# Query-key sums moved from TensorE to accumulating DMAs, and a third GLU block ahead of the down projections

## The chip, the cores and the metric

The kernel runs on one core of a Trainium2 chip. The metric is the device time of one execution in microseconds (us), taken as the median of several executions on the same chip. The profiled execution also has a *span*, from the first to the last instruction, which is about 2 us shorter than the device time of the same execution. Where this text compares stages it uses spans; where it compares kernels it uses device times. The engines are TensorE (PE in the profile; PEld is its weight load), VectorE (DVE), ScalarE (ACT), GpSimd (POOL) and SyncE (SP). POOLq and SPq are the DMA queues that GpSimd and SyncE issue to.

## The reference

One token block of 2048 rows and 640 columns is normalised and then goes through two branches, whose results are added to the input.

```python
def reference(A_x, A_wqkv, A_wo, B_x, B_w_gate, B_w_up, B_w_down):
    xn = layernorm(A_x)                       # [1, 2048, 640], bf16
    # A: 32 heads of 20 columns, a window of 8 keys, 2 apart, backwards
    q, k, v = split_heads(xn @ A_wqkv)        # H = 32, Dh = 20
    idx  = pos[:, None] - 2 * arange(8)       # mask: idx >= 0
    logits = einsum("bhsd,bhswd->bhsw", q, k[idx]) * 20 ** -0.5
    attn = softmax(where(mask, logits, -1e9))
    a = merge_heads(einsum("bhsw,bhswd->bhsd", attn, v[idx])) @ A_wo
    # B: gated linear unit, F = 1536
    b = ((xn @ B_w_gate) * (xn @ B_w_up)) @ B_w_down
    return A_x + a + b                        # B_x is not used
```

## The kernel before

TensorE does the QKV projections, then the GLU products ("gate-up": 4 blocks of 512 rows, each 24 groups of 5 matmuls, 1.08 us a group), then the *down sums*: for 128 rows, twelve matmuls of HT with WD and five of VO with WO into one bank. VectorE does the attention. A head's 20 columns lie as 5 chunks times 4 neighbouring partitions. For each *pair* of window positions (4 pairs for each half of the sequence, 8 in all) VectorE multiplies the 5 chunks of queries and keys, adds two of the five onto two others, and TensorE sums the remaining three chunks and the four partitions with a 0/1 matrix G. ScalarE evicts the result into LOG.

```python
def qk_steps(h, p, s):                        # VectorE, one pair
    kept, tmp = SL[s], TMP                    # kept: 3 chunks, tmp: 2 chunks, 2 window positions each
    ...
    return [(..., prod(kept, 0, NKC)),        # 6144 columns
            (..., prod(tmp, NKC, NCH)),       # 4096 columns
            (..., lambda: ... tensor_tensor(a, a, b, ALU.add))]

def qk_logits(h, batch):                      # TensorE: 12 matmuls a pair
    for p, s in batch:
        for c in range(NKC):
            for q in range(NSB):
                ... e.matmul(o, G[:], x, start=(c == 0), stop=(c == NKC - 1), ...)
    for p, s in batch:
        ... e.activation(o, i, ACT.Copy, scale=SCALE)      # LOG <- PS
    ...
```

Instructions are emitted in program order by a small static scheduler. VectorE's steps are emitted one after the other, and TensorE's "fill" (projections, GLU, down sums) is emitted between them by a modelled clock. The instructions of one engine stand in its queue in the order of emission; waits are inserted from data dependences.

```python
add_gu(0); add_gu(1); add_dn(0); add_gu(2); add_dn(1); add_gu(3); add_dn(2); add_dn(3)   # fill, in this order

batch(0, [pair(0, 0), pair(0, 1)])
batch(0, [pair(0, 2), pair(0, 3)])
headA, restA = softmax_steps(0)               # half A
...
b0 = pair(1, 0)
settle()
for it in headA: step(it)
batch(1, [b0, pair(1, 1)])
for it in restA: step(it)
attn_move(0)
batch(1, [pair(1, 2), pair(1, 3)])            # then WD and WO are loaded over the product buffers
...
pv(0); settle(); headB; pv(1); restB; attn_move(1); pv(2) ... pv(7)   # attention times values, 256 rows each
```

A GLU group of gate and up leaves HT and USX, each evicted from PSUM by ScalarE, and VectorE multiplies HT by USX. There are six USX buffers for this, and six PSUM banks while G needs the other two (eight after the change). If VectorE stands, ScalarE soon has no USX buffer to evict into, and TensorE soon has no bank to write.

## Time and profile before

| | before |
|---|---|
| device time, median of 3 | 262.39 us (262.02 to 262.39) |
| profiled span | 260.7 us |
| TensorE busy | 255.6 us, 98% |
| VectorE busy | 216.1 us, 83% |
| ScalarE busy | 107.3 us, 41% |
| GpSimd busy | 6.7 us, 3% |

The top of the profile page of the kernel before: span, busy time of each engine, and TensorE's busy share in 40 equal slices, in tenths (9 is 90% or more).

```profile
span 260.7 us, 4018 instructions
...
PE 255.6 (98%) x1669; PEld 150.7 (58%) x1669; DVE 216.1 (83%) x240; ACT 107.3 (41%) x193; POOL 6.7 (3%) x13
...
PE   7999999899999999999999999999999999999996
```

TensorE is busy nearly everywhere, so it is taken to be the bound: what is taken from TensorE is gained as long as nothing makes it wait.

TensorE's timeline around the first block of G matmuls (start, duration, engine, line, operation, tiles, count; in brackets the idle time before it and what ended it):

```profile
47.61 0.83 PE L485 MATMUL PS<-SL,G 128*32 128x512 f16 x12
49.35 0.83 PE L485 MATMUL PS<-SL,G 128*32 128x512 f16 x12 [0.91 <-DVE SL L475]
50.11 2.14 PE L424 MATMUL PS<-XNT,WQKV 128*128 128x512 bf16 x9
```

The block takes 50.11 - 47.61 = 2.50 us of TensorE, 0.91 of them idle. The three other blocks of 24 take 1.44, 1.41 and 1.41 us, in all 6.8 us.

Three windows of 10 us (window; its length; busy time and count on PE, PEld, DVE, ACT, POOL; the granted TensorE clock, 1.00 is full; the share of the DMA engines; GB/s):

```profile
100.00:110.00 10.00, 10.00 (x49) 4.51 (x47) 10.00 (x9) 5.66 (x10) 0.00 (x0) 1.00 0.16 50
110.00:120.00 10.00, 10.00 (x65) 4.33 (x64) 9.53 (x11) 5.82 (x11) 0.00 (x0) 1.00 0.71 240
150.00:160.00 10.00, 10.00 (x51) 4.75 (x50) 9.93 (x5) 4.43 (x8) 0.00 (x0) 1.00 0.79 198
```

The one on-chip transfer in the kernel before, in the table of DMA issues (how many, size, median us from issue to landing):

```profile
ATB<-LOG SPq DMA_DIRECT2D x32, 128.0 KB, 2.6
```

### The profile page before, as it was taken

The page shows a single profiled execution, that of the slowest core. Times are in us where ns is not written, and L with a number is a line of the kernel's source. Part 1 is how long each engine was busy: PE and PEld are TensorE (multiplying, and loading weights), DVE is VectorE, ACT ScalarE, POOL GpSimd, SP SyncE. Part 2 cuts the span into 40 slices and gives each one's busy share as a digit, 9 for nine tenths or more (in the row PEclk, how much of TensorE's full clock was granted, in tenths as well). Part 3 has the DMA queues.
Part 4 walks back from the last instruction along what each step waited for, and adds up shares of the span by engine and source line. Part 5 has one row for each costly group of instructions (what it writes and reads, how often), then busy time and mean ns, then how long its engine had stood idle before and what let it go on. Part 6 is the DMA issues. An engine that isn't in the chain of part 4 may idle for free.

```text
span 260.7 us, 4018 instructions
## 1 busy us (share of the span) xinstructions
PE 255.6 (98%) x1669; PEld 150.7 (58%) x1669; DVE 216.1 (83%) x240; ACT 107.3 (41%) x193; POOL 6.7 (3%) x13
## 2 busy tenths in 40 slices
PE   7999999899999999999999999999999999999996
PEld 3899855354554444444467744446774444777775
DVE  5799889999999999998847999999999999422221
ACT  3565558555657555565630035551004555000000
POOL 2000050000200000000000000000000000000000
DMA  6968889400000275065001376000311000021301
GB/s 202 326 136 148 100 226 402 156 3 0 0 3 0 50 206 144 0 208 219 3 0 57 97 199 175 0 4 0 99 54 50 0 3 0 27 74 53 101 28 50
DMA packets 21922, 23.46 MB, mean 90 GB/s; under 512 B 9872, under 2 KB 19472, under 8 KB 21904
## 3 DMA queue, kind: packets, MB, share of 16 engines
q1 hardware_dynamic: 21760, 23.04, 31.2%
q8 instruction: 13, 0.21, 0.3%
q10 hardware_dynamic: 144, 0.16, 0.2%
q14 instruction: 5, 0.04, 0.0%
HBM read 14.42 MB, written 2.62 MB: 65 GB/s over the span
## 4 chain that ended last, share of the span: by engine, by line
PE 80%; DVE 14%; SPq 2%; DMA 2%; ACT 1%; issue 1%
PE PS L577 40%; PE PS L608 28%; PE PS L424 10%; DVE SL L467 3%; SPq L283 2%; DVE XNS L371 2%; PE PS L485 2%; DVE STATS L354 2%; DVE SL L475 2%; DVE TMP L467 2%; DVE STATS L348 2%; DMA XST<-in_A_x_dram 2%; DVE MV L360 1%; DVE SD L369 1%; ACT KH L451 0%
## 5 line engine op out<-in xcount | busy, mean ns | idle before, releaser
L577 PE MATMUL PS<-XNT,WG 128*128 128x512 bf16 x240 | 59.6, 379 | 0.0
L577 PE MATMUL PS<-XNT,WU 128*128 128x512 bf16 x240 | 59.6, 379 | 0.0
L608 PE MATMUL PS<-WD,HT 128*128 128x320 bf16 (+1 forms) x396 | 57.6, 295 | 0.0
L579 ACT ACTIVATE HT<-PS 128x512 bf16<-128x512 f32 x48 | 28.7, 598 | 58.2 <-PE PS L577 58.2
L608 PEld LDWEIGHTS PS<-WD,HT 128*128 128x128 bf16 x396 | 38.1, 98 | 14.7
L551 DVE TENSOR_TENSOR PVB<-VO,ATB 128x10240 f16<-128x10240 bf16 x8 | 43.9, 5488 | 0.1
L424 PE MATMUL PS<-XNT,WQKV 128*128 128x512 bf16 x200 | 43.9, 379 | 0.0
L612 DVE TENSOR_TENSOR FOUT<-PS,XR 128x320 bf16<-128x320 f32 (+1 forms) x33 | 15.5, 477 | 30.4 <-PE PS L608 30.1
L577 PEld LDWEIGHTS PS<-XNT,WU 128*128 128x128 bf16 x240 | 23.4, 98 | 28.5 <-issue 0.4
L577 PEld LDWEIGHTS PS<-XNT,WG 128*128 128x128 bf16 x240 | 23.4, 98 | 28.2 <-issue 0.4
L579 ACT ACTIVATE USX<-PS 128x512 bf16<-128x512 f32 x48 | 28.7, 597 | 22.2 <-PE PS L577 20.8
L424 PEld LDWEIGHTS PS<-XNT,WQKV 128*128 128x128 bf16 x200 | 23.3, 118 | 20.2 <-issue 0.8
L546 DVE TENSOR_TENSOR PVB<-PVB 128x5120 f16<-128x5120 f16 (+1 forms) x16 | 34.4, 2150 | 0.0
L467 DVE TENSOR_TENSOR SL<-QH,KH 128x6144 f16<-128x6144 bf16 x8 | 26.8, 3352 | 1.4 <-ACT KH L451 1.4
L608 PE MATMUL PS<-WO,VO 128*128 128x320 bf16 (+1 forms) x165 | 27.1, 295 | 0.0
L582 DVE TENSOR_TENSOR HT<-HT,USX 128x512 bf16<-128x512 bf16 x48 | 18.5, 417 | 4.2 <-ACT USX L579 4.2
L608 PEld LDWEIGHTS PS<-WO,VO 128*128 128x128 bf16 x165 | 15.9, 98 | 5.9
L475 DVE TENSOR_TENSOR SL<-SL,TMP 128x4096 f16<-128x4096 f16 x8 | 18.3, 2290 | 0.2
L467 DVE TENSOR_TENSOR TMP<-QH,KH 128x4096 f16<-128x4096 bf16 x8 | 18.4, 2302 | 0.0
L430 ACT ACTIVATE VO<-PS 128x512 bf16<-128x512 f32 x20 | 11.9, 597 | 9.8 <-PE PS L424 9.8
L437 PE MATMUL PS<-XNT,WQKV 128*128 128x128 bf16 x200 | 12.6, 220 | 0.2
L437 PEld LDWEIGHTS PS<-XNT,WQKV 128*128 128x128 bf16 x200 | 11.6, 118 | 1.2 <-DVE XNT L394 0.5
(49 smaller groups left out, 137.8 us busy)
## 6 DMA issues: line engine op xcount, KB each, us to landing
ATB<-LOG SPq DMA_DIRECT2D x32, 128.0 KB, 2.6
XR<-in_A_x_dram SPq DMA_DIRECT2D x16, 160.0 KB, 2.3
XST<-in_A_x_dram SPq DMA_DIRECT2D x15, 160.0 KB, 3.9
out_dram<-FOUT SPq DMA_DIRECT2D x15, 160.0 KB, 1.8
WG<-in_B_w_gate_dram SPq DMA_DIRECT2D x1, 1920.0 KB, 9.5
WU<-in_B_w_up_dram SPq DMA_DIRECT2D x1, 1920.0 KB, 13.8
WD<-in_B_w_down_dram SPq DMA_DIRECT2D x1, 1920.0 KB, 8.2
WQKV<-in_A_wqkv_dram SPq DMA_DIRECT2D x10, 160.0 KB, 3.8
```

The source lines that it names most:

```text
L424: op("pe", (lambda l, x, c: lambda e: e.matmul(PS[:, b, :], l, x, start=(c == 0), stop=(c == NCH - 1)))(l, x, c), r=[l, x], w=[PS[:, b, :] ...
L430: op("act", lambda e: e.activation(o, PS[:, b, :], ACT.Copy), r=[PS[:, b, :]], w=[o], name=f"pev{which}_{m}_{j}")
L437: op("pe", (lambda o, l, x, st, sp: lambda e: e.matmul(o, l, x, start=st, stop=sp))(o, l, x, st, sp), r=[l, x], w=[o], name=f"pp{which}_{m ...
L467: return lambda: op("dve", lambda e: e.tensor_tensor(o[:], qw, kw, ALU.mult), r=[q, k], w=[o[:]], name=f"prod{h}_{p}_{c0}")
L475: lambda: op("dve", lambda e: e.tensor_tensor(a, a, b, ALU.add), r=[a, b], w=[a], name=f"psum{h}_{p}")),
L546: return lambda: op("dve", lambda e: e.tensor_tensor(o, x, y, ALU.add), r=[x, y], w=[o], name=f"{name}_{b}")
L551: lambda: op("dve", lambda e: e.tensor_tensor(PVB[:], vw, aw, ALU.mult), r=[v, a], w=[PVB[:]], name=f"pv_{b}")),
L577: op("pe", (lambda l, x, c: lambda e: e.matmul(PS[:, b, :], l, x, start=(c == 0), stop=(c == NCH - 1)))(l, x, c), r=[l, x], w=[PS[:, b, :] ...
L579: op("act", lambda e: e.activation(o, PS[:, b, :], ACT.Copy), r=[PS[:, b, :]], w=[o], name=f"guev{which}_{m}_{j}")
L582: h_pending.append(lambda: op("dve", lambda e: e.tensor_tensor(h, h, o, ALU.mult), r=[h, o], w=[h], name=f"h{m}_{j}"))
L608: op("pe", (lambda l, x, i, b: lambda e: e.matmul(PS[:, b, 0:wid], l, x, start=(i == 0), stop=(i == n - 1)))(l, x, i, b), r=[l, x], w=[PS[ ...
L612: op("dve", (lambda o, xr, b: lambda e: e.tensor_tensor(o, PS[:, b, 0:wid], xr, ALU.add))(o, xr, b), r=[PS[:, b, :], xr], w=[o], name=f"fi ...
```

## The change

The intent is to take the 96 G matmuls off TensorE. Both sums go to the DMA engines. For each pair two accumulating DMAs of 512 KB add the two product sums in a PP buffer onto a third in a PE buffer (these buffers are called PE0 to PE4; they have nothing to do with the engine). Then one plain copy and three accumulating DMAs of 128 KB add the four partition rows of each head into LOG. The six transfers of a pair depend on one another. The Trainium skill says why they must: an accumulating DMA reads its destination and writes it later, and a write that lands in between is lost ("DMA: Bandwidth & Descriptors", Rules for kernel authors). To hide the latency the chains of two neighbouring pairs are interleaved in one issue order. The mask of the first rows becomes an add on VectorE. To give TensorE more work that does not depend on attention, the third GLU block moves ahead of the first down sums, with its HT in columns of the normalised input that are dead by then.

```diff
-            (0.16 + 2 * NKC * HS / 1920, prod(kept, 0, NKC)),
-            (0.16 + 2 * (NCH - NKC) * HS / 1920, prod(tmp, NKC, NCH)),
...
-    def qk_logits(h, batch):
-        ... # 12 matmuls with G a pair, ScalarE evicts into LOG
+        return [prod(first[:], 4), prod(slot[:, 0], 0), prod(slot[:, 1], 1), prod(TMP[:, 0], 2), prod(TMP[:, 1], 3)] + [
+            (2.3, lambda: op("dve", lambda e: e.tensor_tensor(a, a, b, ALU.add), ...)),
+        ]
+
+    def acc(o, i, name):
+        op("pool", lambda e: e.dma_start(o, i, accum_op=ALU.add), r=[o, i], w=[o], dma=True, name=name)
+
+    def qk_chain(h, p, s, en):
+        ...
+            lambda: acc(first[:], slot[:, 0], f"acc{h}_{p}_0"),     # 512 KB
+            lambda: acc(first[:], slot[:, 1], f"acc{h}_{p}_1"),     # 512 KB
+            lambda: dma(dst, row(0), ...),                          # 128 KB, plain, SyncE
+            lambda: acc(dst, row(1), f"row{h}_{p}_1"),              # 128 KB
+            lambda: acc(dst, row(2), f"row{h}_{p}_2"),
+            lambda: acc(dst, row(3), f"row{h}_{p}_3"),
...
+    def chain_stage(new):                     # after each pair: a = its chain, old = the chains before it
+        if a: a.pop(0)()
+        for c in sorted(old, key=len, reverse=True): c.pop(0)()
+        if a: a.pop(0)()
+        for c in old:
+            if len(c) == 2: c.pop(0)()
+        if a: a.pop(0)()
...
+        en = (1, 2, 3, 0, 1, 2, 0, 4)[n]      # which PE buffer; 1, 2 and 3 lie under PVB, the product of attention and values
...
     add_gu(0)
     add_gu(1)
-    add_dn(0)
     add_gu(2)
+    add_dn(0)
+    add_gu(3)
     add_dn(1)
-    add_gu(3)
...
-    b0 = pair(1, 0)
-    settle()
+    pair(1, 0)
+    pair(1, 1)
+    settle(a_end + 22.5)                      # only advances the modelled clock of VectorE
     for it in headA:                          # now begins with the mask add
         step(it)
...
-    batch(1, [pair(1, 2), pair(1, 3)])
+    pair(1, 2)
+    pair(1, 3)
+    drain()                                   # issue what is left of all chains
+    down_loads()                              # WD and WO, over the product buffers PP
+    out_loads()
```

## The prediction

> **What bounds it now.** TensorE. The page gives PE 255.6 of 260.7 us; the table of 10 us windows shows PE at 10.00 of 10.00 from 60 to 250, 48 GLU matmuls per 10 us. VectorE is busy 216.1 us, about 12 us idle between 120 and 150 and little to do after about 222.
>
> **Removed.** The 96 gathering matmuls (G against SL). In the PE timeline the four blocks of 24 displace 1.59, 1.44, 1.41 and 1.41 us (start to next start), plus 0.91 us idle inside the first: 6.8 us, all on the critical path. Also 8 logit evictions on ScalarE, off it. Floor if nothing stalls: 262.4 - 6.8 = 255.6 us.
>
> **Added.** VectorE per pair: five 2048-column products (about 1.22 us each, half of the 4096-column one) and a 2.29 us add: 8.4 us against 7.85 now (pairs start at 33.56, 41.41, 49.21); +4 us over eight pairs, off the path. Per pair, six dependent transfers: two accumulating ones of 512 KB, one plain and three accumulating ones of 128 KB. Plain 128 KB now lands in 2.6 us and 1920 KB in 8.2, so I estimate a plain 512 KB at 3.8. The Trainium skill ("Collectives: The Full Stack", Part 3, The bandwidth ceiling) says that an add needs two source reads and halves the rate, which makes 5 to 6 us each; no trace here shows an accumulating transfer. The same skill ("DMA: Bandwidth & Descriptors", SWDGE vs HWDGE) ties accumulation to GpSimd, so five of six issues stand in one in-order queue, each waiting for its predecessor: about 5.8 + 2.6 + 2 x 0.9 = 10 us per pair (estimate), more than VectorE's 8.4.
>
> **Moved.** Third GLU block ahead of the first down sums: PE has independent work until about 149 instead of 131.
>
> **Critical path after.** GLU starts at about 74. VectorE stops at the mask add until chain A lands; only two gate-up products precede it. Six USX buffers and eight banks let PE run 25 GLU groups, until 74 + 25 x 1.08 = 101. Chain A lands at about 90 if accumulations take 5 us without queueing (the order assumes 22.5 us after pair 4), at about 101 with my 10 us period; every microsecond later stalls PE. Second tight place: WD and WO now lie over the product buffers, so their load waits for the last pair's accumulations, about 135 (147 if queued), plus 8 to 10 us, against PE's first down sum at 149 to 153. Later sums (PV 2 to 7) keep 5 us or more slack by my addition.
>
> **Prediction.** 255.6 plus about 2 us of stalls: 257.6 us, range 254.5 to 267. Faster by over 2% (below 257.1) 0.47; within 2% 0.40; slower 0.13.
>
> **What would show each step.** PE: no G matmuls, busy about 249, idle only near 95 to 110 and 150 to 160. VectorE: one wait at the mask add, released by an accumulating DMA into LOG, ending between 88 and 102. DMA issues: 512 KB accumulations landing in 5 to 6 us, rows in 2.5 to 3. VectorE's pair period 8.4 us for two pairs, then up to 10. WD landed before 155. The chain of waits nearly all PE; GpSimd's queue and DMA in it would say that I am wrong.
>
> **What would make it wrong.** Accumulations of 7 us or more: period over 11 us, chain A at 107 or later, result 264 or more. GpSimd slow at building descriptors (over 1.5 us each) does the same. The first accumulations meet the 4.6 MB of weight loads in flight until about 48. The other way, 4 to 5 us give the full 2.6%.

## The result, and the profile after

| | before | after |
|---|---|---|
| device time, median of 4 | 262.39 us | 274.31 us (273.82 to 276.72) |
| ratio, 95% interval | | 1.0475 (1.0413 to 1.0538) |
| profiled span | 260.7 us | 271.9 us |
| mean granted clock | 1.00 | 0.968 |

A ratio here is the mean time of one kernel's fast runs over that of the other's fast runs of the same rounds, so it is not quite the ratio of the medians. The change made the kernel 4.8% slower, and the time lies above the predicted range.

The page after: the same lines as before, and the granted clock in tenths below TensorE's slices.

```profile
span 271.9 us, 3848 instructions
...
PE 254.9 (94%) x1558; PEld 150.4 (55%) x1573; DVE 216.6 (80%) x265; ACT 100.6 (37%) x185; POOL 38.0 (14%) x52
...
PE   8999999999999971699999699999999999999996
...
PEclk9999999999999996589999799999999999999999
```

A slice is 6.8 us here. TensorE has two holes, at slices 15 to 17 (95 to 116 us) and 23 (150 to 156), and the clock falls at both. The same three windows as before:

```profile
100.00:110.00 10.00, 2.52 (x6) 0.59 (x5) 3.68 (x9) 0.60 (x1) 3.51 (x4) 0.72 0.72 131
110.00:120.00 10.00, 7.47 (x21) 2.88 (x23) 8.32 (x13) 7.71 (x13) 0.00 (x0) 0.59 0.20 74
150.00:160.00 10.00, 8.33 (x30) 3.48 (x32) 10.00 (x12) 6.91 (x14) 1.74 (x2) 0.83 1.04 295
```

TensorE's timeline at the two holes:

```profile
98.96 1.24 PE L589 MATMUL PS<-XNT,WG 128*128 128x512 bf16 x5
107.55 2.31 PE L589 MATMUL PS<-XNT,WU 128*128 128x512 bf16 x5 [7.34 <-ACT USX L591]
112.48 2.31 PE L589 MATMUL PS<-XNT,WG 128*128 128x512 bf16 x5 [2.62 <-ACT HT L591]
114.58 2.34 PE L589 MATMUL PS<-XNT,WU 128*128 128x512 bf16 x5
...
118.51 1.24 PE L589 MATMUL PS<-XNT,WU 128*128 128x512 bf16 x5
...
151.62 1.70 PE L589 MATMUL PS<-XNT,WU 128*128 128x512 bf16 x5 [2.73 <-ACT USX L591]
```

From the start at 98.96 to the start at 118.51 TensorE ran five groups, which take 5 x 1.08 = 5.4 us at full clock. So the first hole cost 19.55 - 5.4 = 14.2 us: 7.34 + 2.62 idle, and the rest at half clock (groups start 2.1 us apart, 112.48 to 114.58, and not 1.08). In the same way four groups between 147.65 and 156.77 cost 9.12 - 4.32 = 4.8 us, of which 2.73 idle. The sum closes to 1 us: 260.7 - 6.8 + 14.2 + 4.8 = 272.9, against a span of 271.9.

The Trainium skill ("TensorE: Matmul & The Clock Gate", Part 1, What's actually happening) says that the array falls to half clock after an idle window of about 3.4 us and returns after about 3.4 us of sustained work. The first hole agrees: 7.34 us idle, then groups of 2.1 us. The second does not quite: the longest idle stretch is 2.73 us and the window still shows a clock of 0.83.

Why TensorE waited is seen on the engines behind it. VectorE's timeline (three of its instructions, the wait in brackets):

```profile
94.22 0.42 DVE L594 TENSOR_TENSOR HT<-HT,USX 128x512 bf16<-128x512 bf16 x1
106.25 0.22 DVE L504 TENSOR_TENSOR LOG<-LOG,MASK 128x112 f16<-128x112 f16 x1 [11.61 <-DMA LOG<-PE]
...
145.04 5.49 DVE L556 TENSOR_TENSOR PVB<-VO,ATB 128x10240 f16<-128x10240 bf16 x1 [8.94 <-DMA LOG<-PE]
```

The mask add, the head of softmax A, waits 11.61 us for the last row of chain A, and the gate-up products that would free USX stand behind it. ScalarE then:

```profile
106.90 0.60 ACT L591 ACTIVATE USX<-PS 128x512 bf16<-128x512 f32 x1 [11.08 <-DVE HT L594]
110.03 1.91 ACT L523 ACTIVATE LOG<-LOG 128x2048 f16<-128x2048 f16 x1 [2.54 <-DVE LOG L521]
```

Evictions stop for 11.08 us, and after one of them the exponential of softmax A stands next in ScalarE's queue. It waits for VectorE's subtract, and the next evictions stand behind it. That is TensorE's second wait, until 112.48. So the logits' late arrival is paid on three in-order queues.

The waits view for VectorE (line, what it waited for: total us, times, longest):

```profile
DVE LOG L504 <- DMA LOG<-PE: 11.6, 1, 11.6
...
DVE PVB L556 <- DMA LOG<-PE: 8.9, 1, 8.9
DVE PP L474 <- DMA PE<-PP: 8.3, 4, 3.6
DVE PE L474 <- DMA LOG<-PE: 3.9, 2, 2.0
```

VectorE loses 11.6 + 8.9 + 8.3 + 3.9 = 32.7 us to these transfers. In the kernel before it lost none to an on-chip transfer.

The chain of waits between 70 and 82 us, in order of time (start, duration, what):

```profile
70.97 5.61 DMA PE<-PP
76.58 0.02 issue
76.60 3.68 DMA LOG<-PE
80.28 0.28 issue
80.56 1.08 POOL LOG L483 x2
```

One loop of 5.61 + 3.68 + 1.08 us and some issue time repeats for each pair. The second accumulation of a pair lands; SyncE's plain row can start; GpSimd's next items in order are two accumulating rows, the first of which needs this plain row; only behind them stands the second accumulation of the next pair, whose data has long been there. The batches of two rows are issued at 69.89, 80.56, 91.94 and 102.61, a period of 10.7 to 11.4 us. VectorE's own work on a pair is shorter: two pairs whose products don't wait start at 117.11 and 126.67, with five gate-up products of about 0.33 us between, which leaves 7.9 us.

By the same issue order the last row of chain A (of pair 3) stands behind the first accumulating row of pair 4, which belongs to half B. Row 2 of pair 3 was issued at 94.89, and a row takes 3.4 us, but its last row was issued only at about 103.15. So half B's chain stands in front of the last row that softmax A needs; no run isolates what this costs.

The same at the second hole, on GpSimd's timeline:

```profile
126.71 0.84 POOL L483 DMA_DIRECT2D PE<-PP  x1 [20.24 <-DVE PP L479]
...
141.41 1.76 POOL L483 DMA_DIRECT2D LOG<-PE  x2 [4.49 <-DMA LOG<-PE]
```

GpSimd stands for 20.24 us because the next item in its queue is the accumulation of pair 6, whose products VectorE has not yet made. By the issue order, the three accumulating rows of pair 5 stand behind it, the last of them also behind the first accumulation of pair 7 and behind a row of pair 6; it is the second of the two rows at 141.41. This matters to VectorE, because the product buffer PVB lies over the PE buffer of pair 5. The 8.94 us wait that ends at 145.04 is for that row.

DMA queue of the software-issued transfers (packets, MB, share of the time of 16 engines) and the landing times:

```profile
q0 software_dynamic: 5760, 11.54, 24.2%
...
PE<-PP POOLq DMA_DIRECT2D x16, 512.0 KB, 5.6
...
LOG<-PE POOLq DMA_DIRECT2D x24, 128.0 KB, 3.4
```

### The profile page after: what moved, and what is told of

It reads as the page before. It is cut to its first block, busy times and chain, and to the rows that moved or that the text cites. A ratio compares the mean times of both kernels' runs of the same rounds, so it can differ in the third digit from the quotient of the medians.

```text
span 271.9 us, 3848 instructions
## 1 busy us (share of the span) xinstructions
PE 254.9 (94%) x1558; PEld 150.4 (55%) x1573; DVE 216.6 (80%) x265; ACT 100.6 (37%) x185; POOL 38.0 (14%) x52
## 3 DMA queue, kind: packets, MB, share of 16 engines
q0 software_dynamic: 5760, 11.54, 24.2%
HBM read 14.42 MB, written 2.62 MB: 63 GB/s over the span
## 4 chain that ended last, share of the span: by engine, by line
PE 41%; DMA 29%; DVE 20%; ACT 2%; SPq 2%; issue 2%; POOL 2%; ACTq 0%
PE PS L620 27%; DMA PE<-PP 17%; PE PS L589 14%; DMA LOG<-PE 11%; SPq L290 2%; DVE PVB L556 2%; DVE XNS L376 2%; DVE STATS L359 2%; POOL LOG L483 2%; DVE HT L594 2%; DVE PP L474 2%; DVE TMP L474 2%; DVE PP L479 2%; DVE STATS L353 2%; DMA XST<-in_A_x_dram 1%
## 5 line engine op out<-in xcount | busy, mean ns | idle before, releaser
L589 PE MATMUL PS<-XNT,WU 128*128 128x512 bf16 x240 | 62.5, 393 | 10.1 <-ACT USX L591 10.1
L620 PE MATMUL PS<-WD,HT 128*128 128x320 bf16 (+1 forms) x300 | 43.2, 294 | 0.0
L620 PEld LDWEIGHTS PS<-WD,HT 128*128 128x128 bf16 x300 | 28.8, 98 | 10.9
L429 PEld LDWEIGHTS PS<-XNT,WQKV 128*128 128x128 bf16 x200 | 23.5, 118 | 19.5
L591 ACT ACTIVATE HT<-PS 128x512 bf16<-128x512 f32 x36 | 21.7, 602 | 26.5 <-PE PS L589 26.5
L483 POOL DMA_DIRECT2D LOG<-PE x24 | 21.5, 992 | 55.2 <-DMA LOG<-PE 55.2
L474 DVE TENSOR_TENSOR PP<-QH,KH 128x2048 f16<-128x2048 bf16 x16 | 19.3, 1224 | 8.3 <-DMA PE<-PP 8.3
L483 POOL DMA_DIRECT2D PE<-PP x16 | 19.1, 1216 | 40.4 <-DVE PP L479 30.1
L474 DVE TENSOR_TENSOR TMP<-QH,KH 128x2048 f16<-128x2048 bf16 x16 | 19.1, 1218 | 0.0
L479 DVE TENSOR_TENSOR PP<-PP,TMP 128x4096 f16<-128x4096 f16 x8 | 18.3, 2292 | 0.2
L436 ACT ACTIVATE VO<-PS 128x512 bf16<-128x512 f32 x20 | 11.9, 597 | 9.6 <-PE PS L429 9.6
L594 DVE TENSOR_TENSOR HT<-HT,USX 128x512 bf16<-128x512 bf16 x36 | 14.2, 417 | 0.0
## 6 DMA issues: line engine op xcount, KB each, us to landing
WU<-in_B_w_up_dram SPq DMA_DIRECT2D x1, 1920.0 KB, 16.2
```

Source lines behind the costliest of these rows:

```text
L429: op("pe", (lambda l, x, c: lambda e: e.matmul(PS[:, b, :], l, x, start=(c == 0), stop=(c == NCH - 1)))(l, x, c), r=[l, x], w=[PS[:, b, :] ...
L436: op("act", lambda e: e.activation(o, PS[:, b, :], ACT.Copy, scale=sc), r=[PS[:, b, :]], w=[o], name=f"pev{which}_{m}_{j}")
L474: return (1.22, lambda: op("dve", lambda e: e.tensor_tensor(o, qw, kw, ALU.mult), r=[q, k], w=[o], name=f"prod{h}_{p}_{c}"))
L479: (2.3, lambda: op("dve", lambda e: e.tensor_tensor(a, a, b, ALU.add), r=[a, b], w=[a], name=f"psum{h}_{p}")),
L483: op("pool", lambda e: e.dma_start(o, i, accum_op=ALU.add), r=[o, i], w=[o], dma=True, name=name)
L589: op("pe", (lambda l, x, c: lambda e: e.matmul(PS[:, b, :], l, x, start=(c == 0), stop=(c == NCH - 1)))(l, x, c), r=[l, x], w=[PS[:, b, :] ...
```

## The experiments

Twelve kernels were run. All were correct but e6. Ratios are to the kernel before in the same rounds; its medians there were 262.2 to 262.4. The column "mask add" is the start of the head of softmax A; "VectorE waits" sums VectorE's waits for on-chip transfers in the waits view of the profiled run. One run each of e7 and e8 counts as slow (over 1.5% above the fastest run of its kernel). It is left out of the ratio but counted in the median.

| run | what | median us | ratio (95%) | span | mask add | VectorE waits |
|---|---|---|---|---|---|---|
| after | the change | 274.31 | 1.0475 (1.0413 to 1.0538) | 271.9 | 106.25 | 32.7 |
| e1_order | another issue order on GpSimd | 270.67 | 1.0341 (1.0305 to 1.0376) | 268.5 | 100.60 | 29.0 |
| e2_drain | rows not held behind pair 6 | 269.51 | 1.0288 (1.0271 to 1.0306) | 266.5 | 106.30 | 27.4 |
| e3_both | e1 and e2 | 264.23 | 1.0083 (1.0058 to 1.0108) | 262.0 | 101.17 | 23.8 |
| e4_warm | dummy matmuls in the first hole | 275.69 | 1.0520 (1.0498 to 1.0542) | 273.4 | 106.90 | 33.3 |
| e5_wu_late | WU loaded later | 274.02 | 1.0430 (1.0413 to 1.0448) | 272.4 | 105.87 | 32.5 |
| e6_plain | copies for adds (wrong result) | 255.60 | 0.9738 (0.9725 to 0.9751) | 253.7 | 88.22 | 9.7 |
| e7_settle | modelled clock only | 282.93 | 1.0734 (1.0683 to 1.0785) | 281.3 | 106.19 | 30.5 |
| e10_settle_ok | eight products ahead of the mask add | 275.89 | 1.0517 (1.0470 to 1.0564) | 272.2 | 106.10 | 28.6 |
| e11_dn_first | third GLU block back | 300.64 | 1.1467 (1.1422 to 1.1512) | 299.0 | 106.74 | 32.9 |
| e8_best | a combination | 260.52 | 0.9914 (0.9879 to 0.9948) | 258.9 | 103.00 | 14.3 |
| e9_best2 | e8, an own buffer, fill ahead | 255.35 | 0.9736 (0.9722 to 0.9751) | 253.3 | 100.96 | 14.6 |
| e12_oneacc | e9, one accumulation a pair | 255.57 | 0.9741 (0.9726 to 0.9755) | 253.5 | 101.80 | 0 |

The first theory was that GpSimd's in-order queue makes the chains late, at two places: between pairs (head of line, chain A) and at pair 5's last rows (chain B). The rivals were that the weight loads make the chains late, that the adding itself is too slow whatever the order, and that the clock costs most of the time.

### e1_order: the order alone

```diff
     def chain_stage(new):        # c1, c2: the chains of one and of two pairs ago
-        ... (see the change)
+        a.pop(0)()               # first accumulation of this pair
+        if c2: c2.pop(0)()       # row 2 of two pairs ago
+        a.pop(0)()               # second accumulation
+        a.pop(0)()               # plain row, SyncE
+        if c2: c2.pop(0)()       # row 3 of two pairs ago
+        if c1: c1.pop(0)()       # row 1 of one pair ago
```

> Only the order of GpSimd's queue changes: no accumulation of a new pair stands behind a row that is not yet due. My theory (head-of-line blocking makes the 10.7 us period; the loop is one 512 KB accumulation, one plain row on SP, two row issues): the pair period falls to about 8.5 to 9.5 us, the mask add is reached by chain A at 94 to 100 instead of 106.3, and the first PE stall (14.2 us lost) shrinks to under 3 us; the second wait, of PV for pair 5's last row, stays. Time 260 to 265. Rival (transfers are slow of themselves, the queue order does not matter; latency of the six dependent transfers is the bound): period stays at 10.5 or more, chain A lands at 104 or later, time 272 to 276.

TensorE's timeline of this run, at its two holes:

```profile
101.90 1.25 PE L589 MATMUL PS<-XNT,WU 128*128 128x512 bf16 x5 [1.71 <-ACT USX L591]
106.83 2.32 PE L589 MATMUL PS<-XNT,WG 128*128 128x512 bf16 x5 [3.68 <-ACT HT L591]
...
147.44 2.31 PE L589 MATMUL PS<-XNT,WU 128*128 128x512 bf16 x5 [4.61 <-ACT USX L591]
```

The period fell from 10.7 to 11.4 us to 9.3 on average (second accumulations issued at 58.01, 66.38, 75.58, 85.44 and 95.22), and the mask add came 5.65 us earlier. The order was therefore a cause of the late chain. But only 3.6 us of device time came back, and the expected 260 to 265 was missed. Counted as above, the first hole shrank from 14.2 to 8.1 us (five groups between 98.95 and 112.45), and the second grew from 4.8 to 7.5 us (four groups between 141.59 and 153.45), where VectorE's wait at PV 0 grew from 8.94 to 10.42 us. So of the 6.1 us that the order won at the first hole 2.7 were lost again at the second. In what is left of the first hole, the second wait is that for ScalarE's exponential, and it comes with the softmax whenever that is. The period did not fall to VectorE's own pair, either. The accumulating rows now overlap with accumulations and take 4.4 us and not 3.4.

### e2_drain: the rows of pair 5 alone

```diff
     pair(1, 1)
+    drain()
     settle(a_end + 22.5)
```

> The rows of pairs 4 and 5 are issued before the softmax of half 0 instead of behind pairs 6 and 7. My theory of the second stall (PV's product buffer lies over the buffers of pairs 0, 1, 2, 4 and 5, and pair 5's last row stands in the queue behind pair 6's): VectorE's 8.9 us wait before the first PV product goes to under 1 us, PE's second stall (4.8 us lost) goes, the first stays. Time about 269.5. Rival (PV waits for the whole chain B, its volume of transfers): the wait stays over 5 us, time 273 or more.

GpSimd's timeline of this run, with the last row of pair 5:

```profile
117.48 0.88 POOL L483 DMA_DIRECT2D LOG<-PE  x1 [2.08 <-DMA LOG<-PE]
```

The row is issued at 117.48 and not after 141. The wait of 8.94 us is gone, and so is the second hole: the window from 150 to 160 has TensorE busy 9.95 us at clock 1.00. The gain is 4.8 us, which is the size counted for that hole. The cause of the second hole is shown.

### e3_both

Both edits together.

> Both edits. My theory: both stalls go but for 0 to 3 us, PE clock 1.00 throughout, time 255.5 to 259, faster than the kernel before by 1.5 to 2.6%. Rival (a serial chain of six transfers cannot be hidden behind 25 GLU groups): still a stall of 8 us or more near 100, time 266 or more.

264.23 us is within 2% of the kernel before. The gain is 10.1 us, more than 3.6 + 4.8 = 8.4, since e1's loss at the second hole is gone as well; but the expectation was missed by 5 us. TensorE still waits 1.75 and 3.68 us near 102 to 107 and then runs at half clock. The mask add still waits 10.86 us at 101.17. The first hole still costs 8.3 us (five groups between 99.47 and 113.21). So the order was not the whole of it.

### e4_warm: is it the clock?

```diff
+            if j == 1 and m == 0: fill.append((0.0, lambda: warm(36)))    # dummy matmuls into a bank of their own
             fill.append((1.08, lambda m=m: glu(0, m, j)))
+            if j == 1 and m == 0: fill.append((0.0, lambda: warm(12)))
             fill.append((1.08, lambda m=m: glu(1, m, j)))
```

> The changed kernel with one PSUM bank fewer in the ring and 36 and 12 dummy matmuls of 512 columns placed where PE idles 7.3 and 2.6 us. Theory: of the 14.2 us lost at the first stall about 10 us are waiting and 4 us are the half clock that follows; with the array kept busy the clock stays above 0.9 from 100 to 120 and the time falls by 3 to 5 us, to about 270. Rival (the lower clock in the records comes of something else, or PE would wait for VectorE anyway): time within 1 us of the changed kernel or above it.

TensorE's timeline of this run at the second hole:

```profile
152.27 2.31 PE L589 MATMUL PS<-XNT,WG 128*128 128x512 bf16 x5 [5.51 <-ACT USX L591]
```

The dummy matmuls did what they should: from 100 to 120 the granted clock is 1.00. But no time came back, against an expectation of about 270. Counted as above, the first hole still cost 13.3 us (three groups between 97.68 and 114.22) and not 14.2: one group fewer ran ahead of it, and the mask add came 0.65 us later. The second cost 7.2 us (three groups between 145.51 and 155.91) and not 4.8. Between 140 and 150 TensorE is busy only 6.70 us, waiting for ScalarE's evictions, which stand behind VectorE's wait at PV 0. The edit also took one PSUM bank away, and its share in this was not separated. So the run does not settle what the half clock costs. It shows that a full clock at the first hole is not enough while VectorE's wait at PV 0 holds TensorE up again.

### e5_wu_late: do the weight loads make the chain late?

```diff
-        for T, src in ((WG, B_w_gate), (WU, B_w_up)):
-            dma(T[:], src.rearrange("(c p) n -> p c n", p=128), ...)
+        dma(WG[:], B_w_gate.rearrange("(c p) n -> p c n", p=128), ...)
...
         pair(0, p)
+        if p == 0:
+            dma(WU[:], B_w_up.rearrange("(c p) n -> p c n", p=128), ...)
```

> The changed kernel with the load of WU issued after the first row instead of at 35 us, so the first two accumulations meet less traffic. Theory (the first accumulation took 8.8 us because of the weight loads): it lands in under 6.5 us, VectorE's first wait for PP (3.6 us) goes, chain A lands 2 to 4 us earlier (about 103), and the time is about 271 to 273. Rival (an accumulation's first use is slow of itself): still over 8 us, same time as the changed kernel.

In the kernel after, the first accumulation took 8.77 us to land. Here the second one is issued at 46.73 and not at 50.55, so the weight load was what slowed the first one. Yet chain A lands at 105.87, only 0.4 us earlier, and the time is unchanged. The load, now issued at 51.94, took 10.5 us and lay beside the next accumulations; VectorE's longest wait for one of them is now 5.6 us and not 3.6. So the edit moved the collision and did not remove it, and how much of chain A's lateness the loads carry is not measured. They do not make the period: in the kernel after WU was issued at 35.03 and landed 16.2 us later, while the batches from 69.89 to 102.61 still came 10.7 to 11.4 us apart.

### e6_plain: is it the adding?

```diff
     def acc(o, i, name):
-        op("pool", lambda e: e.dma_start(o, i, accum_op=ALU.add), ...)
+        op("pool", lambda e: e.dma_start(o, i), ...)
```

The result is wrong (relative error 0.77). Bytes, queues, order and waits are those of the kernel after. Not only the transfers get shorter: an issue holds GpSimd 0.54 us and not 0.88 (in all it is busy 24.4 us and not 38.0). The run does not separate the two.

> A wrong result on purpose: the same transfers, queue and waits, but plain copies instead of adds. Theory as predicted (the second source read makes the transfers slow): 512 KB fall from 5.6 to about 4 us, 128 KB rows from 3.4 to 2.6, the period from 10.7 to 8.5 to 9, chain A at 97 or earlier, time 262 to 266. Rival (fixed latency and the waits make it, the add is nearly free): times to landing within 0.7 us of the accumulating ones, period over 10, time 271 or more.

The software queue and landing times of this run, and the mask add on VectorE's timeline:

```profile
q0 software_dynamic: 3456, 11.54, 11.9%
...
PE<-PP POOLq DMA_DIRECT2D x16, 512.0 KB, 3.1
...
LOG<-PE POOLq DMA_DIRECT2D x24, 128.0 KB, 2.4
```

```profile
88.22 0.22 DVE L504 TENSOR_TENSOR LOG<-LOG,MASK 128x112 f16<-128x112 f16 x1 [5.60 <-DMA LOG<-PE]
```

With copies in place of adds the kernel takes 255.60 us, the predicted floor, with no wait on TensorE in these stages. The expectation of 262 to 266 was missed on the good side: chain A lands at 88.22, and 97 or earlier had been expected. So the order and VectorE's extra work are affordable if the transfers and their issues are short. For the same 11.54 MB the adds hold the DMA engines 24.2% of 271.9 us = 65.8 us, the copies 11.9% of 253.7 = 30.2 us, that is 2.2 times. On average over eight pairs the adds of a pair hold all 16 engines for 65.8 / 8 = 8.2 us, as long as VectorE's own work on a pair (7.9). This agrees roughly with the Trainium skill's page "Collectives: The Full Stack" (Part 3, The bandwidth ceiling), which gives the two source reads of an add as the reason for half the rate; the page measured a ratio of 1.93 between its copying and adding collectives. Why overlapping rows got slower in e1 is open. Fuller DMA engines alone do not explain it: from 52 to 100 us they are busy 0.79 in the kernel after (rows 3.4 us) and 0.90 in e1 (4.4), but only 0.61 in e12, where rows take 4.7.

### e7_settle and e10_settle_ok: put ready products ahead of the wait

The kernel after has two gate-up products shortly before the mask add, one within the last pair's work (at 90.42) and one behind it (94.22). Both runs were to put more of them ahead.

```diff
-    settle(a_end + 22.5)
+    settle(a_end + 34.0)
+    run_fill(t_dve[0])           # only in e10_settle_ok
```

> The changed kernel with one constant: the mask add is placed 34 instead of 22.5 us after pair 4 in the order's own clock, so that VectorE does about six more gate-up products, and ScalarE more evictions before the exp, while chain A is still under way. Transfers are untouched. Theory (the first stall is not the late chain as such but the products and evictions standing behind the wait): chain A lands as before at 104 to 107, but PE idles under 2 us before 120 and its clock stays 1.00 there; a stall of up to 10 us remains between 140 and 160, from PV's wait and WD. Time 263 to 269. Rival (PE stalls because of the chain's latency whatever the order): stall of 8 us or more near 100 stays, time 273 or more.

e7 was a faulty experiment. `settle` only advances the modelled clock; the fill is emitted at the next step, and that is behind the mask add. What the edit did was to move evictions ahead of the exponential on ScalarE, for which VectorE then waited 7.16 us. It says nothing on the theory and was repeated with the missing line.

> e7 done right: in e7 the clock was advanced but no filling work was issued ahead of the mask add, so the products still stood behind it and more evictions stood behind the exp. Here eight gate-up products stand ahead of the mask add; transfers and GpSimd's order are untouched. Theory (the first stall is the order behind the wait, not the lateness of chain A): chain A lands at 104 to 107 as before, PE idles under 2 us between 90 and 120, clock 1.00 there; a stall of 5 to 10 us is left between 140 and 165 (PV's wait and WD). Time 263 to 269. Rival: first stall of 8 us or more stays, time 273 or more.

The window after the mask add in e10, then TensorE at three later places:

```profile
110.00:120.00 10.00, 9.95 (x47) 4.50 (x46) 8.15 (x13) 7.60 (x12) 0.00 (x0) 1.00 0.22 82
```

```profile
157.27 3.36 PE L620 MATMUL PS<-WD,HT 128*128 128x320 bf16 x12 [5.66 <-DMA WD<-in_B_w_down_dram]
...
245.07 0.85 PE L620 MATMUL PS<-WO,VO 128*128 128x320 bf16 x5 [2.57 <-DVE VO L551]
...
260.13 1.51 PE L620 MATMUL PS<-WO,VO 128*128 128x320 bf16 x5 [5.65 <-DVE VO L551]
```

With eight products ahead, chain A is as late as ever (106.10), and the first hole is entirely gone: TensorE has no wait from 90 to 120, at clock 1.00. The expectation of 263 to 269 was missed all the same, with 275.89. The 14 us were given back: TensorE now reaches the first down sum at 151.6 and waits 5.66 us for WD, whose load waits for the last accumulations; later it waits 2.57 and 5.65 us for VectorE's attention results, and around the WD wait the clock falls again (0.80 from 147 to 160). This run is the most informative of the twelve. In the kernel after, TensorE's holes and VectorE's lost 32.7 us lie side by side. Here the first hole was filled while VectorE still lost 28.6 us, and that was worth nothing.

### e11_dn_first: the third GLU block alone

```diff
-    add_gu(2)
     add_dn(0)
+    add_gu(2)
     add_gu(3)
```

> The changed kernel with the third GLU block put back behind the first down sums. Theory (the third block ahead buys PE about 26 us of independent work, and the chain is too late without it): PE waits for PV 0 and WD until about 157, and the time is 282 to 292. Rival (the third block ahead brings nothing or costs): time within 3 us of the changed kernel.

26 us slower than after, more than the expected 282 to 292. TensorE waits 19.52 us for WD at 159.23 and later 7.6 us for VectorE. So the moved block is what keeps WD's lateness from being seen in the kernel after; this half of the change works, and is needed.

### e8_best, e9_best2 and e12_oneacc: is there a version that beats both?

```diff
 # e8: the order of e1, and
+    en = (1, 2, 3, 0, 1, 2, 4, 0)[n]
     pair(1, 1)
+    pair(1, 2); drain()          # more pair work, and all issued rows, ahead of softmax A
+    settle(a_end + 34.0)
     ...
     attn_move(0)
+    down_loads(0)                # first half of WD, while pair 7 is made
     pair(1, 3); drain()
+    down_loads(1)
     ...
+    settle(b_end + 24.0)         # was 20.0; before softmax B
 # e9: e8, and
+    PE_.append(sb("PE5", PSB, FP16)); en = (1, 2, 3, 0, 1, 2, 4, 5)[n]   # room from NXR = 2 and from MSK0 laid over USX
+    run_fill(t_dve[0])           # after settle
```

> A version meant to beat both: order of GpSimd's queue as in e1, drain as in e2, the mask add placed 34 us after pair 4, pair 7 (first of the last two) ahead of the softmax of half 0 with the buffers of pairs 7 and 8 swapped, WD loaded in two halves, the first before the last pair. Theory: PE idles under 2 us after 10 us, clock 1.00, time 254.5 to 258, ratio 0.97 to 0.985. Rival (VectorE, now near 100% busy after the waits, becomes the bound): VectorE busy to the end and PE waits for PV 6 and 7 between 220 and 250, time 259 or more.

e8 came to 260.52 us, within 2% of the kernel before and above the expected 254.5 to 258. TensorE still waited 3.54 us for WO at 156.44, whose load was issued at 152.19, behind the last row of the last pair.

> As e8, with the last pair's first-product buffer in 4 KB of its own (one residual buffer fewer, the mask source laid over another buffer), so that the load of WO no longer waits for the last row; and the filling work is now really placed ahead of the mask add. Theory: the 3.5 us wait for WO at 153 and the lower clock after it go, PE has no wait over 1 us after 10 us, time 255.3 to 257.5, at the floor of 255.6. Rival (VectorE behind: the waits of e8 move to the PV sums of the last tiles): time 258 or more, PE idle between 160 and 250.

The page of e9 and its mask add:

```profile
span 253.3 us, 3851 instructions
...
PE 249.1 (98%) x1558; PEld 149.5 (59%) x1573; DVE 216.5 (85%) x265; ACT 103.0 (41%) x185; POOL 37.7 (15%) x52
...
PE   8999999999999999999999999999999999999996
```

```profile
100.96 0.22 DVE L506 TENSOR_TENSOR LOG<-LOG,MASK 128x112 f16<-128x112 f16 x1 [0.64 <-DMA LOG<-PE]
```

255.35 us, correct, 2.6% faster than the kernel before and 6.9% faster (255.35 / 274.31) than the kernel after by medians. Chain A lands at about 101, no earlier than in e1 (the accumulations are as slow as ever, 5.0 and 4.2 us for the rows), but VectorE has pair work and products ahead of the wait, so that it waits 0.64 us. The parts of e8 and e9 were not tried one by one, so which of them is dispensable stays open.

For e12 one of the two accumulations was taken away: VectorE adds its two halves itself (1.22 us a pair), and the chain has five steps, with the issue order adapted to it.

> As e9, with one 512 KB accumulation per pair instead of two: VectorE adds the other half itself (1.22 us more per pair, about 10 us in all). Theory (the accumulating transfers keep the DMA engines about 8.2 us per pair, which is as long as VectorE's pair; with half of the large ones the chain stops being the bound): rows land in 3.5 us or less, VectorE's waits for DMA in the pairs go under 2 us in all, PE as in e9, time 255.3 to 258. Rival (VectorE's added 10 us delay the last PV sums): time 259 or more.

255.57 us, within the noise of e9. VectorE has no wait left for these transfers, and the software queue holds 17.3% of the DMA engines. TensorE is the bound in both, so nothing is gained. The rows did not get faster (4.7 us, where 3.5 or less had been expected); why is open.

## Why the prediction was wrong

What held:

- *The floor.* 6.8 us of TensorE removed gives 255.6. e6 (255.60) and e9 (255.35) reach it, so TensorE was the bound before. TensorE's busy time at full clock is 249.1 us in e9, where about 249 had been predicted.
- *The 512 KB accumulation.* 5 to 6 us predicted, 5.6 measured. In part this was luck: the estimate started from 3.8 us for a plain 512 KB copy, which took 3.1 in e6, so the copy was put too high and the price of adding too low.
- *How far TensorE gets.* It was predicted to run out of work at 101; its last group before the hole started at 98.96 and ran 1.24 us.
- *The mechanism.* GpSimd's in-order queue was predicted to set a period of about 10 us for a pair, more than VectorE needs; it was 10.7 to 11.4. Only the mask add, with two products ahead of it, was named as the place where the chain is waited for.
- *The WD load, nearly.* Issue by 147 if queued, plus 8 to 10 us; it was issued at 148.56 and landed at about 158.6, later than the 155 given as a test. In the kernel after TensorE is too late to see it, in e10 it costs 5.66 us.

What failed:

- *The landing of chain A*, "at about 101 with my 10 us period", was 106.25. Two terms were too small. The plain row, the one row that is in the loop, took 3.5 to 3.7 us and not 2.6, and one accumulation took 6.5 us, so three periods lasted 32.7 us and not 30. And the first accumulation took 8.8 us under the weight loads. e1 moved the landing to 100.60 by the order alone; e5 moved the weight load onto the next accumulations and won 0.4 us, so the share of this second term is open.
- *The price of lateness*, "every microsecond later stalls PE". The mask add came 5.2 us after the predicted 101, and TensorE lost 14.2. The rest is the exponential, which stands between two evictions on ScalarE and makes TensorE wait a second time, and the half clock after the wait. e1 and e3 show that part by itself: the chain on time as predicted (100.6 and 101.2), and still 1.7 + 3.7 us of waiting and about 8 us lost at the first hole. Thus even the predicted landing would not have given "about 2 us of stalls".
- *A place that was not seen.* Idle time near 150 to 160 had been predicted, but from WD; it came at 147 to 157 from another cause. PVB lies over the PE buffers of pair 5, and pair 5's last row stands behind the accumulations of pairs 6 and 7. It cost 4.8 us; e2 gives them back.
- *"Later sums (PV 2 to 7) keep 5 us or more slack."* The addition took VectorE as never standing, and its slack as larger than it was: the prediction says about 12 us idle between 120 and 150 in the kernel before, where the windows of 10 us show 9.02, 4.91 and 8.96 us busy, so 7.1 idle. In the kernel after it lost 32.7 us, and e10 shows that once the first hole is filled TensorE waits 2.57 and 5.65 us for the later sums.

The step that failed is "255.6 plus about 2 us of stalls". The stalls were 14.2 + 4.8 = 19 us, and 255.6 + 19 = 274.6, against 274.31 measured. The slack was counted only as independent work in front of TensorE, and the chain's length was slightly under-sized. What the runs showed in its place is that a late transfer was paid on four in-order queues (GpSimd's, VectorE's, ScalarE's, TensorE's), and that VectorE's lost time was a second bound at about the same height. That the adds are the root, by their transfers or their issues, is shown by e6; that the kernel could have afforded them in another order is shown by e9. The prediction had written that a result of 264 or more would come with "chain A at 107 or later", and this nearly came true (106.25, 274.31) from a period of about 11, though by other terms than the one it named: the 512 KB accumulations took 5.6 us, not 7.

## What to carry to other kernels

In this kernel accumulating DMAs held the DMA engines 2.2 times as long as copies of the same bytes. A chain of such transfers was hidden only where no in-order queue had ready work standing behind an item of the chain that was not ready: look at every queue that the late data passes, and put the ready work ahead of the wait. When the bound engine gets slack, add up the waits of the second-busiest engine too. Here it was worth nothing to fill TensorE's first hole while VectorE still waited 28.6 us (e10); with VectorE's waits down to 14.6 us as well, the floor was reached (e9). Before spending a gain, run the cheap impossible version, such as copies in place of adds, to see what is left to win.

## What the Trainium skill lacked or had wrong

- "DMA: Bandwidth & Descriptors" says that accumulation goes only through GpSimd (SWDGE vs HWDGE vs iDMA), and the traces agree in that all adds here stand on POOLq; but it has no duration for an accumulating transfer from SBUF to SBUF. Measured: 512 KB 5.6 us against 3.1 for the copy, 128 KB 3.4 against 2.4, and 4.2 to 4.7 for 128 KB where they overlap with others.
- The factor for an add stands only in "Collectives: The Full Stack", for collectives (1.93). For local accumulating DMAs the DMA page should have it: 65.8 against 30.2 us of 16 engines for the same 11.54 MB, 2.2 times, with 5760 packets against 3456.
- No page says what an accumulating issue costs GpSimd. Its issues show 0.84 to 0.88 us each where one stands alone; plain ones of the same shape (e6) 0.54 on average.
- "TensorE: Matmul & The Clock Gate" gives about 3.4 us of idleness for the fall to half clock. Here the mean clock of a window fell to 0.83 after an idle stretch of 2.73 us (the second hole of the kernel after). Whether the page's free-running window explains this (idle stretches on both sides of a short burst) no run here shows.
